# The order of the early second stage and the place of the last weight sums in a fused attention and bilinear kernel

## The chip, the cores and the metric

The kernel runs on one core of a Trainium2 chip. The metric is the device time of one execution in microseconds (us). The profile shows the core's engines: PE (TensorE matmuls), PEld (TensorE weight loads, which overlap the matmuls), DVE (VectorE), ACT (ScalarE), POOL (GpSimd, nearly unused here) and SP (SyncE, which here only issues DMA transfers).

## The reference, cut to what matters

```python
def _attn_ref(x, state):            # x: 8 x 8 x 512 x 64, state: 8 x 8 x 32 x 64
    scores = scale * np.matmul(x, state.transpose(0, 1, 3, 2))
    a = softmax(scores)
    xread = np.matmul(a, state)
    scores2 = scale * np.matmul(state, x.transpose(0, 1, 3, 2))
    a2 = softmax(scores2)
    sread = np.matmul(a2, x)
    return np.concatenate([xread, sread], axis=2)

def _moe_ref(x, w1, w2, w3, w_out):  # x: 4608 x 512
    a = x @ w1
    b = x @ w2
    h = a * b @ w3
    return h @ w_out
```

`softmax` stands for the four lines that subtract the maximum, take the exponential and divide by the sum. Inputs other than `x` and `state` arrive as float64 bits in parts of the program that the change leaves alone.

## The kernel before

All work on one batch of 512 tokens goes through two stages. **Stage 1** works feature tile by feature tile (`FT` = 8 tiles of 128 features): `stage1_sums` issues twelve matmuls on line 311, six for each of the two weight matrices, into a pair of PSUM banks. Then ACT copies one bank out (line 487, or 292 in batch 0), DVE multiplies the copy by the other bank (line 394, or 293), and the product is split into a high and a low part (`split`: ACT line 97 for the high part, DVE line 98 for the low part). That product is what frees the two banks. **Stage 2** multiplies the products by `w34` = w3 w_out, which is kept as `wo["hi"]` and `wo["lo"]`, three matmuls for each pair of tiles (high by low, high by high, low by high).

PSUM has eight banks. Two single banks (`bank()`, tile `ps_o`) serve stage 2. Three pairs (`two_banks()`, tile `ps`) serve stage 1, the attention scores and the w units; a tile of a pool takes a place that an older tile of the same name has left, and waits until the last reader of that tile is done.

Batch 0 runs beside the set-up that converts the weights. Its stage 2 goes by four token tiles of 128. Two of them are taken early: `early_stage2(quarter)` accumulates two feature tiles into `acc[0]` and `acc[1]` (`project`, line 325), in between the feature tiles of stage 1. After that the loop over `tt` stores the two early ones (`store`: ACT line 338 copies a bank out, a DMA sends it) and works out the other two with `stage2`.

Batches 1 to 7 (`quarter_batch`) use a fast scheme for stage 2: seven products of quarters in place of eight, which need sums and differences of blocks of `w34` (the w sums). `combine_weights(k)` makes a quarter of them: two sums on DVE (line 366), four differences into a scratch tile `raw` (line 372), then a split into `t_hi` (ACT line 97) and `t_lo` (DVE line 98). The sums take their scratch from `tmp`, a ring of four buffers that the copies out of PSUM use too. The products of these batches differ from batch 0's: `hidden_quarters` multiplies on line 394 and takes a difference on line 405. Beside stage 1, batch b also works on the attention of batch b + 1: scores (PE line 147), a transpose (DVE line 187), the maximum (line 190), and the softmax.

Two things set the order. PE and SP are scheduled by hand for the whole kernel: their instructions stand as the code issues them. ACT and DVE are scheduled by hand only up to `order.close()`, that is, through the set-up. Behind it a scheduler orders these two by the priority in which the code was written and by its estimate of when inputs are ready; blocks under `tc.high_priority()` (the copies and products of stage 1 and the stores) go ahead. On the chip each engine then runs its instructions in the order of the program. Last of all come the state rows (`state_rows`) of all batches.

Of the kernel before, what the change touches and what calls it, by code (L numbers as in the profile page):

```python
# [36 lines left out]
PLAIN = 1  # L37

@with_exitstack
def attn_bilinear_kernel(  # L40
# [11 lines left out]
    B, _, NT, H, D = x_s.shape  # L52
# [35 lines left out]
    def bank():  # L88
        return ps_o.tile([P, NF], F32, name="ps_o")

    def two_banks():
        return ps_2.tile([P, 2, NF], F32, name="ps_2")

    def split(hi, lo, src):

        return (
            nc.scalar.copy(out=hi, in_=src),  # L97
            nc.vector.tensor_tensor(out=lo, in0=src, in1=hi.bitcast(F32), op=ALU.subtract),  # L98
        )
# [165 lines left out]
    def sw_steps(b):  # L265
        sw_tiles.setdefault(b, {})

        def unit(half, i):
            ps = two_banks()
            as_q = ps.rearrange("p k (c f) -> p k c f", c=2)  # L270
            per_head(as_q, b, lambda rows, j: w_sb[rows, 2 * half:2 * half + 2, i, j])
            sw_tiles[b][half, i] = sw_pair()
            split(*sw_tiles[b][half, i], ps)

        return [(lambda half=half, i=i: unit(half, i)) for half in range(HALF) for i in range(2)]
# [26 lines left out]
    def stage1_sums(b, ft):  # L302
        half, c = divmod(ft * P, NF)
        ps = two_banks()
        hi, lo = at_tiles[b]
        for i in range(2):
            w_hi, w_lo = sw_tiles[b][half, i]
            k = 0
            for kt in range(KT):
                for w, a in ((w_hi, lo), (w_hi, hi), (w_lo, hi)):  # L310
                    nc.tensor.matmul(  # L311
                        ps[:, i], w[:, kt, c:c + P], a[:, kt], start=(k == 0), stop=(k == 3 * KT - 1)
                    )
                    k += 1
        return ps
# [43 lines left out]
    QF = FT // 2  # L359
    HT, HO = S // 2, DO // 2  # L360

    def combine_weights(k):

        raw = [tmp_tile() for _ in range(2)]
        for i, whole in enumerate(raw):
            nc.vector.tensor_tensor(
                out=whole, in0=wo["hi"][:, i * QF + k].bitcast(F32), in1=wo["lo"][:, i * QF + k].bitcast(F32), op=ALU.add
            )
        b11, b12, b21, b22 = (whole[:, half * HO:(half + 1) * HO] for whole in raw for half in range(2))
        t = late.tile([P, QF, S], F32, name="raw")[:, :, :HO]  # L370
        for j, (x, y) in enumerate(((b12, b11), (b22, t[:, 0]), (b22, b12), (b21, t[:, 1]))):
            nc.vector.tensor_tensor(out=t[:, j], in0=x, in1=y, op=ALU.subtract)
        split(t_parts["hi"][:, :, k], t_parts["lo"][:, :, k], t)

    def tmp_tile():
        return main.tile([P, NF], F32, name="tmp", bufs=4)
# [102 lines left out]
    def quarter_batch(b):  # L479
        q = {"raw": []}  # L480
        w = sw_steps(b + 1) if b + 1 < B else [lambda: None] * 4
        softmax = iter(())
        for ft in range(FT):
            ps = stage1_sums(b, ft)
            a_sb = tmp_tile()
            with tc.high_priority():
                nc.scalar.copy(out=a_sb, in_=ps[:, 0])  # L487
            hidden_quarters(a_sb, ps[:, 1], ft, q)
            if ft == 1:
                run([reads[b]])  # L490
                if b + 1 < B:
                    scores, reads[b + 1], _ = attention_steps(b + 1)
                    softmax = scores()
                    next(softmax)
                    load_tokens(b + 1)
                if b + 2 < B:
                    load_x(b + 2)
            elif ft in (2, 4):
                next(softmax, None)
            if b == PLAIN and ft == 1:  # L500
                combine_weights(QF - 1)
        stage2_quarters(b, q, w[:2], [*w[2:], lambda: softmax])

    def run(steps):
# [5 lines left out]
    with tc.tile_pool(name="pro", bufs=2) as pro:  # L510

        places = [w_sb[:, n // 2, n % 2].rearrange("p j f -> p (j f)") for n in range(2 * QT)]
        w_out = [places[(FT + k) // 2][:, k % 2 * DO:(k % 2 + 1) * DO] for k in range(FT)]

        chunks = [places[k % (FT // 2)] for k in range(FT)]
        w3s, w34_ps = {}, {}

        def finish(i):
            split(wo["hi"][:, i], wo["lo"][:, i], w34_ps[i][:, :DO])

        def convert_first(k):
            ends = PARTS.get(k, (NW,))
            return to_f32(pro, w34_k[k], chunks[k], ends, (), wout=w_out[k])

        def w34_first(k):

            for i in range(FT // 2):
                nc.tensor.matmul(
                    w34_ps[i][:, :DO], chunks[k][:, DO + i * P:DO + (i + 1) * P], w_out[k],
                    start=(k == 0), stop=(k == FT - 1),  # L530
                )

        def convert_w3(i):
            w3s[i] = pro.tile([P, NW], F32, name="w3", bufs=2)
            return to_f32(pro, w3t[i - FT // 2], w3s[i])

        def w34(i, ks=range(FT)):
            if ks[0] == 0:
                w34_ps[i] = bank()
            for k in ks:  # L540
                nc.tensor.matmul(
                    w34_ps[i][:, :DO], w3s[i][:, k * P:(k + 1) * P], w_out[k], start=(k == 0), stop=(k == FT - 1)
                )

        def convert_half(n):

            return to_f32(pro, w12[n], places[n])

        def sets(quarter):
            for i in range(2):  # L550
                sw_quarter(0, quarter, i)


        gs, acc, early = [], [], range(2)

        def early_stage2(quarter):
            for tt in early:
                if quarter == 0:
                    acc.append(bank())
                for ft in range(2 * quarter, 2 * quarter + 2):  # L560
                    project(acc[tt], gs, tt, ft)

        order = ctx.enter_context(ExitStack())
        order.enter_context(tc.manual_schedule(engines={mybir.EngineType.Activation, mybir.EngineType.DVE}))
        pair = two_banks()
        w34_ps.update(enumerate([bank(), bank(), pair[:, 0], pair[:, 1]]))
        for k in range(FT + AHEAD):
            run([partial(convert_first, k) if k < FT else partial(convert_w3, k - FT // 2)])
            if k >= AHEAD:
                w34_first(k - AHEAD)  # L570
        load_x(0)
        scores, reads[0], _ = attention_steps(0)
        softmax = scores()
        next(softmax)
        finish(0)
        finish(1)
        split(wo["hi"][:, 2:4], wo["lo"][:, 2:4], pair[:, :, :DO])
        w34(4)

        w1_0, w2_0, w1_1, w2_1 = map(convert_half, range(4))  # L580
        go = lambda steps: next(steps, None)
        w3_6 = convert_w3(6)
        go(w1_0), go(softmax), go(w1_0)
        finish(4)
        go(w2_0), go(w3_6), go(softmax), go(w3_6)
        w34(5)
        go(softmax)
        go(w2_0)
        finish(5)
        w3_7 = convert_w3(7)  # L590
        go(w3_7), go(w3_7), go(w1_1), go(w1_1), go(w2_1), go(w2_1)
        load_tokens(0)
        w34(6)
        sets(0)
        finish(6)
        w34(7, range(LAST))
        sets(1)
        w34(7, range(LAST, FT))
        finish(7)
        order.close()  # L600
        for quarter in range(QT):
            stage1(0, 2 * quarter, gs)
            if quarter == 1:
                run(sw_steps(0)[2:])
            if quarter:
                early_stage2(quarter - 1)
            if quarter == 1:
                side = side_steps()
            elif quarter == 2:
                run(side.pop(0))  # L610
            stage1(0, 2 * quarter + 1, gs)
            if quarter == 0:
                run([partial(convert_half, n) for n in range(4, 2 * QT)])
                load_x(1)
                with tc.issue_after(last_split[1].ins):
                    go(softmax)
        run(side.pop(0))
        early_stage2(QT - 1)
# [3 lines left out]
    for tt in range(NT):  # L622
        dests = [(out[0, tt * P:(tt + 1) * P], 0, P)]
        if tt in early:
            store(acc[tt], dests)
        else:
            stage2(gs, tt, dests)
        run(side[tt])
        if tt + 1 < QF:
            combine_weights(tt)  # L630

    def state_rows():
        n = B * NS
# [74 lines left out]
```

## Time and profile before

| what | us |
|---|---|
| median of 3 runs (lowest, highest) | 494.64 (494.48, 495.07) |
| the profiled execution | 494.89 |
| its span | 493.1 |
| PE busy | 486.8 |
| DVE busy | 375.9 |
| ACT busy | 238.8 |
| batch 1 begins on PE, from the span's start | 120.29 |
| batch 2 begins on PE | 169.40 |
| batch 3 begins on PE | 218.05 |

The span is the time between the first and last instruction that the profiler saw; the device time holds a little more around it. All starts below are counted from the span's start. A row of a timeline gives start, duration, engine, line, operation, output <- inputs, shapes and count; brackets give idle time ahead of the instruction, and what ended it. Matmuls overlap each other, so that a matmul's own duration is longer than the step from one start to the next.

### The profile page before, as it was taken

What the parts mean: (1) busy time and instruction counts of PE and PEld (TensorE: products, weight loads), DVE (VectorE), ACT (ScalarE), POOL (GpSimd) and SP (SyncE); (2) the same over time, 40 slices, a digit from 0 to 9 for tenths busy, and PEclk for the clock granted to TensorE, in tenths of its full rate; (3) what the DMA queues carried; (4) which work ended last, traced back from release to release, by engine and by line L of the source; (5) the groups of instructions that cost most, each with busy time, mean ns of one, the idle gap of its engine ahead of it and who ended that gap; (6) DMA issues with size and microseconds to landing.
All of it is one profiled execution on the core that took longest, in us unless ns stands there. A gap on an engine that the chain in (4) does not pass through costs nothing.

```text
span 493.1 us, 8917 instructions
## 1 busy us (share of the span) xinstructions
PE 486.8 (99%) x3558; PEld 378.4 (77%) x3558; DVE 375.9 (76%) x555; ACT 238.8 (48%) x364; POOL 0.2 (0%) x4
## 2 busy tenths in 40 slices
PE   8999999999999999999999999999999999999996
PEld 6444467777787978797889778977897788899885
DVE  5669897699899579937994899389839983577870
ACT  4777784444357135704560456055505650354650
POOL 0000000000000000000000000000000000000000
PEclk9999999999999999999999999999999999999999
DMA  8996981153113504130413042304220222001001
GB/s 342 359 394 216 366 294 25 19 183 97 34 51 132 128 5 179 39 90 5 179 41 91 5 177 46 85 5 177 49 82 6 87 49 80 6 2 55 33 1 43
DMA packets 56362, 52.50 MB, mean 106 GB/s; under 512 B 42752, under 2 KB 50944, under 8 KB 51712
## 3 DMA queue, kind: packets, MB, share of 16 engines
q1 hardware_dynamic: 47488, 43.27, 26.9%
q10 hardware_dynamic: 8832, 8.65, 5.1%
q8 instruction: 28, 0.46, 0.4%
q14 instruction: 14, 0.11, 0.1%
HBM read 38.27 MB, written 8.91 MB: 96 GB/s over the span
## 4 chain that ended last, share of the span: by engine, by line
PE 77%; DMA 7%; DVE 7%; ACT 5%; SPq 2%; issue 1%; DVEq 0%; ACTq 0%
PE ps L311 30%; PE ps_o L421 25%; PE ps L147 6%; PE ps_o L325 5%; PE ps L421 4%; DMA raw<-in_w_k_dram 3%; PE ps L647 3%; ACT ulps L126 2%; SPq L171 2%; DMA raw<-in_w_dram 2%; PE ps L648 2%; DMA raw<-in_w3t_dram 2%; PE ps_o L243 1%; ACT w_sb L118 1%; DVE work L187 1%
## 5 line engine op out<-in xcount | busy, mean ns | idle before, releaser
L311 PE MATMUL ps<-at_lo,sw_hi 128*128 128x512 f32 x256 | 101.9, 398 | 0.3 <-DVE g_x L394 0.3
L311 PE MATMUL ps<-at_hi,sw_hi 128*128 128x512 f32 x256 | 99.8, 390 | 0.0
L311 PE MATMUL ps<-at_hi,sw_lo 128*128 128x512 f32 x256 | 99.7, 389 | 0.0
L487 ACT COPY tmp<-ps 128x512 f32<-128x512 f32 x56 | 32.8, 587 | 124.5 <-PE ps L311 70.1
L311 PEld LDWEIGHTS ps<-at_lo,sw_hi 128*128 128x128 f32 x256 | 48.1, 188 | 18.7 <-DVE g_x L394 8.1
L311 PEld LDWEIGHTS ps<-at_hi,sw_lo 128*128 128x128 f32 x256 | 48.1, 188 | 10.2
L311 PEld LDWEIGHTS ps<-at_hi,sw_hi 128*128 128x128 f32 x256 | 48.1, 188 | 9.5 <-issue 0.2
L394 DVE TENSOR_TENSOR g_x<-tmp,ps 128x512 f32<-128x512 f32 x28 | 19.1, 683 | 33.3 <-ACT tmp L487 32.8
L98 DVE TENSOR_TENSOR sw_lo<-ps,sw_hi 128x1024 fp32r<-128x1024 f32 (+1 forms) x34 | 38.1, 1154 | 0.2 <-ACT sw_hi L97 0.2
L97 ACT CAST g_hi<-g_x 128x512 fp32r<-128x512 f32 x42 | 26.0, 621 | 21.2 <-PE ps_o L421 13.1
L421 PE MATMUL ps_o<-t_lo,g_hi 128*128 128x256 f32 x168 | 34.5, 287 | 0.0
L421 PE MATMUL ps_o<-wo_lo,g_hi 128*128 128x256 f32 x168 | 34.4, 286 | 0.0
L421 PE MATMUL ps_o<-wo_hi,g_hi 128*128 128x256 f32 x168 | 33.8, 283 | 0.0
L421 PE MATMUL ps_o<-t_hi,g_hi 128*128 128x256 f32 x168 | 33.8, 283 | 0.0
L421 PE MATMUL ps_o<-wo_hi,g_lo 128*128 128x256 f32 x168 | 33.8, 283 | 0.0
L421 PE MATMUL ps_o<-t_hi,g_lo 128*128 128x256 f32 x168 | 33.8, 283 | 0.0
L97 ACT CAST g_hi<-raw 128x512 fp32r<-128x512 f32 x42 | 25.2, 619 | 16.5 <-DVE raw L394 7.8
L98 DVE TENSOR_TENSOR g_lo<-raw,g_hi 128x512 fp32r<-128x512 f32 x42 | 28.8, 689 | 4.6 <-ACT g_hi L97 4.3
L97 ACT CAST sw_hi<-ps 128x1024 fp32r<-128x1024 f32 (+1 forms) x34 | 31.2, 967 | 1.7 <-PE ps L147 1.6
L147 PE MATMUL ps<-w_sb,st 64*32 64x512 f32 (+1 forms) x544 | 31.4, 570 | 0.0
L421 PEld LDWEIGHTS ps_o<-wo_lo,g_hi 128*128 128x128 f32 x168 | 26.6, 191 | 5.6 <-ACT tmp L446 5.0
L421 PEld LDWEIGHTS ps_o<-t_lo,g_hi 128*128 128x128 f32 x168 | 26.1, 192 | 5.0 <-issue 5.0
(109 smaller groups left out, 895.8 us busy)
## 6 DMA issues: line engine op xcount, KB each, us to landing
raw<-in_w_k_dram SPq DMA_DIRECT2D x8, 1024.0 KB, 6.9
x_d<-in_x_d_dram SPq DMA_DIRECT2D x8, 1024.0 KB, 7.5
raw<-in_w_dram SPq DMA_DIRECT2D x8, 1024.0 KB, 6.8
x_s<-in_x_s_dram SPq DMA_DIRECT2D x8, 1024.0 KB, 5.0
out_dram<-tmp ACTq DMA_DIRECT2D x56, 128.0 KB, 1.8
raw<-in_w3t_dram SPq DMA_DIRECT2D x4, 1024.0 KB, 7.6
e<-work SPq DMA_DIRECT2D x112, 32.0 KB, 2.0
sread<-turned SPq DMA_DIRECT2D x128, 4.0 KB, 1.7
```

The source lines that it names most:

```text
L97: nc.scalar.copy(out=hi, in_=src),
L98: nc.vector.tensor_tensor(out=lo, in0=src, in1=hi.bitcast(F32), op=ALU.subtract),
L126: nc.scalar.activation(out=ulps[:, part], in_=low.bitcast(U32), func=AF.Copy, scale=2.0**-29)
L147: nc.tensor.matmul(ps[j * NS:(j + 1) * NS, q], sts[b][rows, j], moving(rows, j), start=True, stop=True)
L171: nc.sync.dma_start(out=dest(slice(c * NS, (c + 1) * NS), j), in_=src(slice(j * NS, (j + 1) * NS), c))
L311: nc.tensor.matmul(ps[:, i], w[:, kt, c:c + P], a[:, kt], start=(k == 0), stop=(k == 3 * KT - 1))
L325: nc.tensor.matmul(ps[:, :DO], g, wo[w][:, ft, :], start=(ft == 0 and k == 0), stop=(ft == FT - 1 and k == 2))
L394: nc.vector.tensor_tensor(out=whole, in0=a, in1=b, op=ALU.mult)
L421: nc.tensor.matmul(ps[:, tt * HO:(tt + 1) * HO], g[:, tt * P:(tt + 1) * P], w(part, k), start=(fresh and k == 0 and n == 0 and tt == 0), s ...
L487: nc.scalar.copy(out=a_sb, in_=ps[:, 0])
L647: nc.tensor.matmul(ps[:, i], wh[:, ks], sr[:, kt], start=(kt == 0), stop=False)
L648: nc.tensor.matmul(ps[:, i, :n], wl[:, ks], sr[:, kt, 1], start=False, stop=(kt == NP - 1))
```

## The change

The change has two edits. In `early_stage2` the loop over the two token tiles goes inside the loop over feature tiles, and both banks are taken ahead of the loops. And `combine_weights(QF - 1)`, the last quarter of the w sums, which was called in batch 1 behind feature tile 1, is called in the loop over token tiles of batch 0, where the other three quarters are.

```diff
@@ quarter_batch
             elif ft in (2, 4):
                 next(softmax, None)
-            if b == PLAIN and ft == 1:
-                combine_weights(QF - 1)
         stage2_quarters(b, q, w[:2], [*w[2:], lambda: softmax])
@@ early_stage2
         def early_stage2(quarter):
-            for tt in early:
-                if quarter == 0:
-                    acc.append(bank())
-                for ft in range(2 * quarter, 2 * quarter + 2):
+            if quarter == 0:
+                acc.extend(bank() for _ in early)
+            for ft in range(2 * quarter, 2 * quarter + 2):
+                for tt in early:
                     project(acc[tt], gs, tt, ft)
@@ the loop over token tiles of batch 0
         run(side[tt])
-        if tt + 1 < QF:
-            combine_weights(tt)
+        combine_weights(tt)
```

On PE, feature tiles 4 and 5 in early stage 2. `ps_o_544` is `acc[0]`; `ps_o_551` before and `ps_o_545` after are `acc[1]`. `g_hi_591` and `g_lo_592` are the parts of tile 4, `g_hi_652` and `g_lo_653` those of tile 5. Before, up to the first reader of `g_lo_653`:

```order
L325 MATMUL ps_o_544<-wo_lo_94,g_hi_591 128x512
L325 MATMUL ps_o_544<-wo_hi_93,g_hi_591 128x512
L325 MATMUL ps_o_544<-wo_hi_93,g_lo_592 128x512
L325 MATMUL ps_o_544<-wo_lo_94,g_hi_652 128x512
L325 MATMUL ps_o_544<-wo_hi_93,g_hi_652 128x512
L325 MATMUL ps_o_544<-wo_hi_93,g_lo_653 128x512
```

And now, on the same engine at the same place:

```order
L325 MATMUL ps_o_544<-wo_lo_94,g_hi_591 128x512
L325 MATMUL ps_o_544<-wo_hi_93,g_hi_591 128x512
L325 MATMUL ps_o_544<-wo_hi_93,g_lo_592 128x512
L325 MATMUL ps_o_545<-wo_lo_94,g_hi_591 128x512
L325 MATMUL ps_o_545<-wo_hi_93,g_hi_591 128x512
L325 MATMUL ps_o_545<-wo_hi_93,g_lo_592 128x512
L325 MATMUL ps_o_544<-wo_lo_94,g_hi_652 128x512
L325 MATMUL ps_o_544<-wo_hi_93,g_hi_652 128x512
L325 MATMUL ps_o_544<-wo_hi_93,g_lo_653 128x512
```

The first reader of `g_lo_653` moved from the sixth matmul to the ninth.

On PE, tiles 6 and 7 in early stage 2 (`g_x_672` and `g_x_703`, each holding both parts) and the first matmul of token tile 2 (`ps_o_865`, which takes the bank of `ps_o_544`). Before:

```order
L325 MATMUL ps_o_544<-wo_lo_94,g_x_672 128x512
L325 MATMUL ps_o_544<-wo_hi_93,g_x_672 128x512 x2
L325 MATMUL ps_o_544<-wo_lo_94,g_x_703 128x512
L325 MATMUL ps_o_544<-wo_hi_93,g_x_703 128x512 x2
L325 MATMUL ps_o_551<-wo_lo_94,g_x_672 128x512
L325 MATMUL ps_o_551<-wo_hi_93,g_x_672 128x512 x2
L325 MATMUL ps_o_551<-wo_lo_94,g_x_703 128x512
L325 MATMUL ps_o_551<-wo_hi_93,g_x_703 128x512 x2
L325 MATMUL ps_o_865<-wo_lo_94,g_hi_420 128x512
```

And now:

```order
L325 MATMUL ps_o_544<-wo_lo_94,g_x_672 128x512
L325 MATMUL ps_o_544<-wo_hi_93,g_x_672 128x512 x2
L325 MATMUL ps_o_545<-wo_lo_94,g_x_672 128x512
L325 MATMUL ps_o_545<-wo_hi_93,g_x_672 128x512 x2
L325 MATMUL ps_o_544<-wo_lo_94,g_x_703 128x512
L325 MATMUL ps_o_544<-wo_hi_93,g_x_703 128x512 x2
L325 MATMUL ps_o_545<-wo_lo_94,g_x_703 128x512
L325 MATMUL ps_o_545<-wo_hi_93,g_x_703 128x512 x2
L325 MATMUL ps_o_865<-wo_lo_94,g_hi_420 128x512
```

The last matmul into `ps_o_544` moved from the sixth place to the ninth of twelve, three ahead of the matmul that needs its bank instead of six.

On DVE, the first products of batch 1. `ps_2_958` and `ps_2_983` are feature tiles 0 and 1, `ps_2_1084` is tile 2, `ps_2_1058` the scores; `raw_923` belongs to the third quarter of the w sums and `raw_1077` to the last. Before, the stretch around tile 2's product:

```order
L366 TENSOR_TENSOR tmp_1073<-wo_hi_93,wo_lo_94 128x512
L366 TENSOR_TENSOR tmp_1074<-wo_hi_93,wo_lo_94 128x512
L372 TENSOR_TENSOR raw_1077<-tmp_1073 128x256
L372 TENSOR_TENSOR raw_1077<-tmp_1074,tmp_1073 128x256
L372 TENSOR_TENSOR raw_1077<-tmp_1074,raw_1077 128x256
L187 STREAM_TRANSPOSE work_1101<-ps_2_1058 128x1024
L394 TENSOR_TENSOR g_x_1099<-tmp_1097,ps_2_1084 128x512
L372 TENSOR_TENSOR raw_1077<-tmp_1074,raw_1077 128x256
L190 TENSOR_REDUCE m2_1103<-ps_2_1058 128x2
L98 TENSOR_TENSOR t_lo_795<-raw_1077,t_hi_794 128x4x256
```

And now, from the third quarter's `t_lo` on, where `ps_2_969` and `ps_2_994` are tiles 0 and 1 and `raw_962` belongs to the last quarter; its first sum (into `tmp_958`) stands just ahead of this piece:

```order
L98 TENSOR_TENSOR t_lo_795<-raw_923,t_hi_794 128x4x256
L366 TENSOR_TENSOR tmp_959<-wo_hi_93,wo_lo_94 128x512
L372 TENSOR_TENSOR raw_962<-tmp_958 128x256
L372 TENSOR_TENSOR raw_962<-tmp_959,tmp_958 128x256
L394 TENSOR_TENSOR g_x_984<-tmp_982,ps_2_969 128x512
L372 TENSOR_TENSOR raw_962<-tmp_959,raw_962 128x256 x2
L98 TENSOR_TENSOR t_lo_795<-raw_962,t_hi_794 128x4x256
L394 TENSOR_TENSOR g_x_984<-tmp_1007,ps_2_994 128x512
```

The last quarter's sums moved from behind the product of tile 1 to ahead of it, its `t_lo` with them. The transpose on line 187, the reduction on line 190 and tile 2's product now follow each other in this order. In the built program tile 4 of batch 1 takes the banks of tile 2 in both kernels; tile 5 takes those of tile 3 before, and those of the scores now.

## The prediction

> **What bounds the kernel now.** I read the page's busy times first, then the chain that ended last, then the waits of PE (TensorE) alone.
>
> ```profile
> PE 486.8 (99%) x3558; PEld 378.4 (77%) x3558; DVE 375.9 (76%) x555; ACT 238.8 (48%) x364; POOL 0.2 (0%) x4
> PE 77%; DMA 7%; DVE 7%; ACT 5%; SPq 2%; issue 1%; DVEq 0%; ACTq 0%
> PE ps_o L325 <- DVE g_lo L98: 0.3, 1, 0.3
> PE ps L311 <- DVE g_x L394: 0.3, 1, 0.3
> ```
>
> PE is the bound. Its work is the same before and after the change, so only its waits count. Behind the set-up the view of waits shows two, and each edit touches one: line 325 waits for a low part in early stage 2, and line 311 waits for a product in batch 1. A DVE or ACT instruction that moves costs nothing until PE waits for it. The chain in order of time shows what the second wait is worth:
>
> ```profile
> 120.29 5.45 PE ps L311 x24
> 169.40 5.47 PE ps L311 x24
> 218.05 5.46 PE ps L311 x24
> ```
>
> These are the starts of batches 1, 2 and 3. Batch 1 takes 49.11 us and batch 2 48.65, so batch 1 loses 0.46 more than a steady batch. The last row also gives PE's step: 24 matmuls in 5.46 us are 0.2275 us from start to start.
>
> **The first edit: tiles outermost in early stage 2.** The timelines of PE and DVE at feature tiles 4 and 5:
>
> ```profile
> 96.12 0.40 PE L325 MATMUL ps_o<-wo_hi,g_hi 128*128 128x512 f32 x1
> 96.85 0.50 PE L325 MATMUL ps_o<-wo_hi,g_lo 128*128 128x512 f32 x1 [0.34 <-DVE g_lo L98]
> 97.19 0.39 PE L325 MATMUL ps_o<-wo_lo,g_hi 128*128 128x512 f32 x1
> 96.11 0.68 DVE L98 TENSOR_TENSOR g_lo<-tmp,g_hi 128x512 fp32r<-128x512 f32 x1
> ```
>
> The matmul at 96.12 is the fifth of twelve. The sixth needs the low part of tile 5, which DVE ends at 96.79. From 96.12 to 97.19 there should be two steps, 0.455, but there are 1.07: the stop costs 0.61, of which 0.11 is the slower restart (0.34 from the first matmul to the second). After the change the low part of tile 5 is first read by the ninth matmul, at 96.12 + 4 × 0.2275 = 97.03, behind 96.79. **Gain 0.61.**
>
> The same edit moves the end of the first accumulator. At tiles 6 and 7:
>
> ```profile
> 104.13 0.65 DVE L98 TENSOR_TENSOR g_x<-tmp,g_x 128x512 fp32r<-128x512 f32 x1
> 104.29 0.50 PE L325 MATMUL ps_o<-wo_lo,g_x 128*128 128x512 f32 x1
> 107.14 0.39 PE L325 MATMUL ps_o<-wo_lo,g_hi 128*128 128x512 f32 x1
> 106.04 0.59 ACT L338 COPY tmp<-ps_o 128x512 f32<-128x512 f32 x1 [0.50 <-PE ps_o L325]
> ```
>
> The row at 107.14 opens token tile 2 in the bank that `acc[0]` leaves. `acc[0]` was complete after six of twelve matmuls, and its copy ended at 106.63, 0.51 before that row. Now it is complete after nine, 3 × 0.2275 = 0.68 later, and the slack of 0.51 becomes a wait of 0.17, with a restart 0.28. **Loss 0.28**: a bank takes the place of the low part. The low part of tile 7 (104.13 + 0.65 = 104.78) is first read by the seventh matmul instead of the fourth; even 0.61 earlier that is 104.29 + 0.11 + 6 × 0.2275 - 0.61 = 105.15, so nothing stops there. Net, PE comes out of batch 0 0.33 us earlier. If the ACT copy were later for another reason, all of the 0.33 could go; if it came at once, 0.61 would stay.
>
> DVE gains less. Its product of tile 7 waited for a copy that PE's lateness delayed:
>
> ```profile
> 100.80 1.23 DVE L216 TENSOR_TENSOR work<-work,sum 128x1024 f32<-128x1024 f32 x1
> 102.17 0.69 DVE L293 TENSOR_TENSOR tmp<-tmp,ps 128x512 f32<-128x512 f32 x1
> 101.55 0.59 ACT L292 COPY tmp<-ps 128x512 f32<-128x512 f32 x1 [2.61 <-PE ps L311]
> ```
>
> The copy ended at 102.14, now 101.53. An operation on 1024 columns lets the next one start 1.14 us after it (the row at 134.78 and the one behind it, below), so the product can start at 101.94: **0.23 earlier**, no more, and DVE then works almost without a gap. The bounds are 0 and 0.61.
>
> **The second edit: the last quarter of the w sums.** It removes and adds no instruction; it moves four microseconds of DVE work ahead of batch 1's products. The order of instructions decides the rest. Before, on DVE, ACT and PE:
>
> ```profile
> 119.72 0.68 DVE L366 TENSOR_TENSOR tmp<-wo_hi,wo_lo 128x512 f32<-128x512 f32 x1
> 120.32 0.76 DVE L372 TENSOR_TENSOR raw<-tmp 128x256 f32<-128x256 f32 x2
> 122.99 1.23 DVE L98 TENSOR_TENSOR t_lo<-raw,t_hi 128x1024 fp32r<-128x1024 f32 x1 [1.12 <-ACT t_hi L97]
> 124.52 0.69 DVE L394 TENSOR_TENSOR g_x<-tmp,ps 128x512 f32<-128x512 f32 x1 [0.30 <-ACT tmp L487]
> 126.38 0.69 DVE L394 TENSOR_TENSOR g_x<-tmp,ps 128x512 f32<-128x512 f32 x1 [1.17 <-ACT tmp L487]
> 132.68 0.65 DVE L394 TENSOR_TENSOR g_x<-tmp,ps 128x512 f32<-128x512 f32 x1
> 133.25 0.41 DVE L372 TENSOR_TENSOR raw<-tmp,raw 128x256 f32<-128x256 f32 x1
> 133.58 1.22 DVE L190 TENSOR_REDUCE m<-ps 128x2 f32<-128x1024 f32 x1
> 134.78 1.23 DVE L98 TENSOR_TENSOR t_lo<-raw,t_hi 128x1024 fp32r<-128x1024 f32 x1
> 135.92 0.68 DVE L394 TENSOR_TENSOR g_x<-tmp,ps 128x512 f32<-128x512 f32 x1
> 133.05 0.39 PE L311 MATMUL ps<-at_hi,sw_lo 128*128 128x512 f32 x1
> 133.39 0.50 PE L311 MATMUL ps<-at_lo,sw_hi 128*128 128x512 f32 x1
> 136.66 0.50 PE L311 MATMUL ps<-at_lo,sw_hi 128*128 128x512 f32 x1 [0.26 <-DVE g_x L394]
> 137.00 0.40 PE L311 MATMUL ps<-at_hi,sw_hi 128*128 128x512 f32 x1
> ```
>
> The four rows of line 394 are the products of tiles 0 to 3, and each frees two banks. Tile 4 of PE starts at 133.39, 0.06 behind the end of tile 2's product; tile 5 at 136.66, 0.06 behind tile 3's. In the changed program tile 4 again takes the banks of tile 2, while tile 5 takes those of the scores. So the deciding time is the end of tile 2's product, 132.68 + 0.65 = 133.33 before. Three things move it:
>
> - Ahead of it now stand the last `raw` difference, the reduction on line 190 and the last `t_lo`, which stood behind it: 0.33 + 1.13 + 1.14 = 2.60 later (the reduction at the 1.13 of its size, since the `t_lo` behind it was itself waiting).
> - DVE's idle time ahead of it was 1.12 + 0.30 + 1.17 = 2.59. Now the first w sum of the last quarter stands in the 1.12 (0.60, from 119.72 to 120.32) and leaves 0.52; the 0.30 and the 1.17 are filled with work. But the last conversion has the chain of the third, differences on DVE, `t_hi` on ACT, `t_lo` on DVE, with nothing queued between: 1.12 again. Idle left 1.64, so 0.95 earlier.
> - DVE itself comes 0.23 earlier.
>
> 133.33 + 2.60 - 0.95 - 0.23 = 134.75, and PE starts tile 4 at 134.81. Without a wait it would be there at 133.05 + 0.23 - 0.33 = 132.95: a wait of nearly 1.9 us, which swallows the gain of the first edit whole. Behind the waiting matmul stand all of PE's later matmuls. Tile 5 follows at 134.81 + 0.11 + 12 × 0.2275 = 137.65 without a wait, if the scores' banks are free by then. ACT's exponentials read them last:
>
> ```profile
> 137.17 0.68 ACT L197 ACTIVATE e<-ps,m 128x512 f32<-128x512 f32 x1
> 138.41 0.20 ACT L197 ACTIVATION_READ_ACCUMULATOR e<-ps,m 128x1 f32 x1
> ```
>
> The pair takes 1.44 us. In the changed order it waits only for the small operation behind tile 2's product, so it ends near 136.3, ahead of 137.65. Before, tile 5 ran as if from 137.00 - 0.23 = 136.77. **Net +0.88 us.** Behind it neither kernel waits in batch 1, DVE has the sums behind it, and the later batches keep their 48.65.
>
> Bounds: were the sum not to fit into the 1.12 (0.60) and DVE not earlier (0.23), +1.71. Were the second 1.12 covered by other work, -0.24.
>
> **Sum.** The profiled execution took 494.89 us (span 493.1), 0.25 above the median of 494.64. 494.89 + 0.88 = 495.77; against the median 495.52. I take 495.5. A change under 0.2% (0.99 us) can't be told from none here.
>
> **Rivals.**
>
> *Batch 1 becomes a steady batch (faster).* There tile 4 hardly waits:
>
> ```profile
> 182.57 0.50 PE L311 MATMUL ps<-at_lo,sw_hi 128*128 128x512 f32 x1
> 181.84 0.67 DVE L394 TENSOR_TENSOR g_x<-tmp,ps 128x512 f32<-128x512 f32 x1
> ```
>
> In batch 2 PE also starts 0.06 behind the product of tile 2. Without the sums in its midst batch 1 could fall to 48.65: -0.46 and -0.33 make -0.79, 493.85 by the median. It needs tile 2's product done by 132.9, 1.85 earlier than I count; DVE's order speaks against it, since the last `t_lo` stands between the products of tiles 0 and 1. Chance 0.14, 0.05 of it beyond 0.2%.
>
> *The two sides cancel.* If DVE is 0.9 less late, the loss is nil: 494.6. Chance 0.07. The first edit failing in its own place belongs to the forecast, for its gain is swallowed: +1.11 (DVE not earlier).
>
> *The wait of nearly 1.9 us slows PE's clock (slower).* Its place is tile 4 of batch 1.
>
> ```profile
> 130.00:140.00 10.00, 9.74 (x43) 7.46 (x42) 10.00 (x15) 4.86 (x10) 0.00 (x0) 1.00 0.05 7
> ```
>
> The granted clock (third number from the end) stayed 1.00 over the stop at 136.66, a third of this one. At half the clock, tile 4's twelve matmuls alone would take 12 × 0.2275 = 2.73 more: +3.61, 498.25. It decides from where a stop is long enough; no row has one of this length. Chance 0.05. The Trainium skill ("TensorE: Matmul & The Clock Gate", section "A second HAM failure mode: psum-queue depth-cycling") speaks against such a change: short idle times of PE between groups that cycle through PSUM banks made its clock fall back in another kernel. By its Part 1 the drop takes an idle window of about 3.4 us; by that the clock stays.
>
> **How the numbers follow.** Forecast 0.74, reaching from 494.4 to 496.35 (-0.24 to +1.71); its centre of 0.88 is near 0.99, so 0.32 of it is slower by over 0.2% and 0.42 within. With the rivals: faster 0.05, within 0.42 + 0.09 + 0.07 = 0.58, slower 0.32 + 0.05 = 0.37. The range 494.3 to 496.4 leaves out the first rival and the clock, 0.19.
>
> **What would show it.** Right: no wait of line 325 for the low part of tile 5; a stop of about 0.3 at the first matmul of token tile 2, behind ACT line 338; a stop of 1.5 to 2 us at tile 4 of batch 1, behind line 394; none at tile 5; batch 2 starting about 0.9 later than 169.40. Wrong: line 394 of tile 2 ending before 133.5, DVE idle under 1 us ahead of the last `t_lo`, or a later batch longer than 48.65.

## The result and the profile after

| kernel | median us | lowest, highest | runs |
|---|---|---|---|
| before | 494.57 | 494.01, 495.53 | 19 |
| after | 495.37 | 494.96, 496.46 | 19 |

The ratio is 1.0015, with a 95% interval from 1.0008 to 1.0021: the change costs 0.8 us. That is less than the 0.2% (0.99 us) below which the prediction counts a change as none, but more than nothing, since the interval leaves out 1. The forecast was 495.5. The profiled execution of the kernel after took 495.37 us, with a span of 493.6.

The page's busy times and the view of PE's waits, of the kernel after (a wait's row gives the total, the number of times and the longest, in us):

```profile
PE 486.7 (99%) x3558; PEld 378.4 (77%) x3558; DVE 376.0 (76%) x555; ACT 239.0 (48%) x364; POOL 0.2 (0%) x4
PE ps L311 <- DVE g_x L394: 1.1, 1, 1.1
```

The busy times are those of before. The wait of line 325 for the low part has left the list, and that of line 311 for a product has grown from 0.3 to 1.1 us; it is now the wait of another tile. The chain in order of time, of the kernel after (start, duration, what):

```profile
134.35 11.18 PE ps L311 x48
169.81 5.47 PE ps L311 x24
218.47 5.47 PE ps L311 x24
```

The chain now enters batch 1's first stage at 134.35, tile 4, and not at 136.66, tile 5. Batch 2 starts 0.41 later than before (169.81 against 169.40), and the steady batch still takes 48.66. That is less than the 0.8 of the medians, because the two profiled executions differ already in the set-up; the one before took 494.89, 0.32 above its median. A DVE reduction in batch 0 that stands ahead of every stop that the change touches shows by how much:

```profile
92.09 1.19 DVE L190 TENSOR_REDUCE m<-ps 128x2 f32<-128x1024 f32 x1
91.73 1.19 DVE L190 TENSOR_REDUCE m<-ps 128x2 f32<-128x1024 f32 x1
```

The first row is before, the second after: DVE was 0.36 earlier in the second execution. This row is the **DVE mark** below. Counted from it, batch 2 starts 0.41 + 0.36 = 0.77 us later, in line with the medians.

The first edit, in the timelines of PE and DVE of the kernel after:

```profile
96.62 0.39 PE L325 MATMUL ps_o<-wo_hi,g_hi 128*128 128x512 f32 x1
96.85 0.39 PE L325 MATMUL ps_o<-wo_hi,g_lo 128*128 128x512 f32 x1
95.76 0.69 DVE L98 TENSOR_TENSOR g_lo<-tmp,g_hi 128x512 fp32r<-128x512 f32 x1
105.88 0.61 PE L325 MATMUL ps_o<-wo_hi,g_x 128*128 128x512 f32 x2
105.91 0.59 ACT L338 COPY tmp<-ps_o 128x512 f32<-128x512 f32 x1 [1.15 <-PE ps_o L325]
106.54 0.50 PE L325 MATMUL ps_o<-wo_lo,g_hi 128*128 128x512 f32 x1
106.88 0.40 PE L325 MATMUL ps_o<-wo_hi,g_hi 128*128 128x512 f32 x1
```

The first reader of tile 5's low part is the ninth matmul, at 96.85; the part is ready at 95.76 + 0.69 = 96.45, and PE keeps its even step. At the hand-over ACT's copy of `acc[0]` ends at 106.50, and the first matmul of token tile 2 starts at 106.54 in place of 105.88 + 2 × 0.2275 = 106.33: a stop of 0.21 and a restart of 0.11 (0.34 to the second matmul instead of 0.2275).

The second edit, in the timeline of DVE and then of PE:

```profile
122.41 1.23 DVE L98 TENSOR_TENSOR t_lo<-raw,t_hi 128x1024 fp32r<-128x1024 f32 x1 [0.52 <-ACT t_hi L97]
124.82 0.68 DVE L394 TENSOR_TENSOR g_x<-tmp,ps 128x512 f32<-128x512 f32 x1
127.41 1.23 DVE L98 TENSOR_TENSOR t_lo<-raw,t_hi 128x1024 fp32r<-128x1024 f32 x1 [1.11 <-ACT t_hi L97]
128.56 0.68 DVE L394 TENSOR_TENSOR g_x<-tmp,ps 128x512 f32<-128x512 f32 x1
132.52 1.19 DVE L190 TENSOR_REDUCE m<-ps 128x2 f32<-128x1024 f32 x1
133.63 0.67 DVE L394 TENSOR_TENSOR g_x<-tmp,ps 128x512 f32<-128x512 f32 x1
132.84 0.39 PE L311 MATMUL ps<-at_hi,sw_lo 128*128 128x512 f32 x1
134.35 0.50 PE L311 MATMUL ps<-at_lo,sw_hi 128*128 128x512 f32 x1 [1.12 <-DVE g_x L394]
134.69 0.39 PE L311 MATMUL ps<-at_hi,sw_hi 128*128 128x512 f32 x1
137.20 0.39 PE L311 MATMUL ps<-at_lo,sw_hi 128*128 128x512 f32 x1
```

The idle times ahead of the two `t_lo` are 0.52 and 1.11. The product of tile 2 ends at 134.30. PE would have begun tile 4 at 132.84 + 0.23 = 133.07 and begins at 134.35, a stop of 1.28 and a restart of 0.11. (The bracket gives 1.12, since it counts from the end of the matmul ahead, which is modelled.) Tile 5 follows at 137.20 without a wait.

### The profile page after: what moved, and what is told of

Read it like the earlier page. It is cut to its first block, busy times and chain, and to the rows that moved or that the text cites. A ratio compares the mean times of both kernels' runs of the same rounds, so it can differ in the third digit from the quotient of the medians.

```text
span 493.6 us, 8920 instructions
## 1 busy us (share of the span) xinstructions
PE 486.7 (99%) x3558; PEld 378.4 (77%) x3558; DVE 376.0 (76%) x555; ACT 239.0 (48%) x364; POOL 0.2 (0%) x4
## 4 chain that ended last, share of the span: by engine, by line
PE 78%; DVE 11%; ACT 5%; DMA 3%; SPq 2%; issue 1%; ACTq 0%; DVEq 0%
PE ps L311 29%; PE ps_o L421 25%; PE ps L147 6%; PE ps L421 4%; PE ps L644 3%; PE ps_o L526 3%; PE ps L526 3%; PE ps_o L325 2%; SPq L171 2%; PE ps L645 2%; ACT ulps L126 1%; DMA raw<-in_w_dram 1%; ACT w_sb L118 1%; PE ps_o L243 1%; DVE raw L372 1%; DMA raw<-in_w_k_dram 1%
```

## The experiments

All results in one place; "before" is the kernel before on the same chip. The ratio is that of the comparison with before and need not equal that of the two medians. The last two columns are from each kernel's profile and count to the first matmul of batch 2 (169.24 before, 169.65 after; the chain's rows above start 0.16 behind it). One counts from the DVE mark, the other from the first matmul of batch 1 (120.12 before, 119.70 after). The first is the right measure where DVE decides when batch 2 starts, the second where PE does. The changed kernel was measured in one session and is compared below with runs of others; the kernel before agrees in all of them within 0.1.

| kernel | median us (runs) | before | ratio, 95% interval | DVE mark to batch 2 | batch 1 to batch 2 |
|---|---|---|---|---|---|
| before | | 494.57 | | 77.15 | 49.12 |
| after | 495.37 (19) | 494.57 | 1.0015, 1.0008 to 1.0021 | 77.92 | 49.95 |
| first edit alone | 494.68 (11) | 494.59 | 0.9999, 0.9991 to 1.0008 | 77.19 | 49.12 |
| the same again | 494.43 (11) | 494.57 | 1.0005, 0.9996 to 1.0013 | 76.96 | 49.12 |
| second edit alone | 495.63 (11) | 494.59 | 1.0017, 1.0009 to 1.0026 | 78.20 | 50.12 |
| after, tiles 6 and 7 in the old order | 495.32 (11) | 494.59 | 1.0025, 1.0013 to 1.0038 | 77.93 | 50.37 |
| after, last split later | 494.63 (11) | 494.59 | 0.9997, 0.9988 to 1.0006 | 76.81 | 49.02 |
| after, scores later | 494.25 (11) | 494.49 | 0.9999, 0.9990 to 1.0007 | 76.90 | 48.84 |
| after, a reduction twice | 495.45 (11) | 494.49 | 1.0018, 1.0009 to 1.0027 | 77.90 | 50.11 |
| first edit, tiles 6 and 7 in the old order | 494.04 (11) | 494.57 | 0.9993, 0.9984 to 1.0002 | 76.59 | 49.13 |
| before, reduction behind tile 2 | 493.18 (7) | 494.49 | 0.9968, 0.9957 to 0.9979 | 77.17 | 49.11 |
| after, three things together | 491.91 (5) | 494.49 | 0.9948, 0.9935 to 0.9960 | 76.32 | 48.32 |

**The second edit alone.** The early second stage goes back to the old order:

```diff
-            if quarter == 0:
-                acc.extend(bank() for _ in early)
-            for ft in range(2 * quarter, 2 * quarter + 2):
-                for tt in early:
+            for tt in early:
+                if quarter == 0:
+                    acc.append(bank())
+                for ft in range(2 * quarter, 2 * quarter + 2):
                     project(acc[tt], gs, tt, ft)
```

> The second edit alone: early stage 2 goes token tiles outermost as before. Theory, that DVE's order decides and PE's gain from the first edit is swallowed: the wait for the low part of tile 5 in early stage 2 is back (0.6 us on PE), the product of tile 2 in batch 1 ends only 0.23 later than in the changed kernel, the stop ahead of tile 4 of batch 1 is about 0.1 shorter than there, and the time is 0.2 us above the changed kernel (495.6 against 495.37; +1.0 to +1.1 against before). Rival, that PE's sum counts in full: 0.33 above the changed kernel (495.7).

Measured: 495.63, 0.26 above the changed kernel; from the mark, 0.28. The two ratio intervals overlap, so the medians alone don't show the 0.26; and it lies between the 0.23 of DVE and the 0.33 of PE, and by itself tells neither. The timelines of DVE and then of PE, of this kernel:

```profile
100.83 1.22 DVE L216 TENSOR_TENSOR work<-work,sum 128x1024 f32<-128x1024 f32 x1
102.25 0.69 DVE L293 TENSOR_TENSOR tmp<-tmp,ps 128x512 f32<-128x512 f32 x1 [0.19 <-ACT tmp L292]
96.89 0.50 PE L325 MATMUL ps_o<-wo_hi,g_lo 128*128 128x512 f32 x1 [0.41 <-DVE g_lo L98]
135.02 0.50 PE L311 MATMUL ps<-at_lo,sw_hi 128*128 128x512 f32 x1 [1.50 <-DVE g_x L394]
```

DVE's product of tile 7 starts 102.25 - 100.83 = 1.42 behind the operation ahead of it, since it waits for the copy again; in the changed kernel the two starts are 1.15 apart (100.44 and 101.59). So the first edit brings DVE 0.27 here, and that is the whole 0.28 from the mark. On PE the wait of early stage 2 is back. The stop at tile 4 is longer than in the changed kernel, not the 0.1 shorter that was expected: in this execution the product of tile 2 came 0.66 later (0.40 at the mark, 0.27 from tile 7), and PE's last matmul of tile 3 only 0.29 later (133.13 against 132.84).

**Tiles 6 and 7 in the old order.** In the changed kernel, the last quarter of early stage 2 goes token tiles outermost:

```diff
-            for ft in range(2 * quarter, 2 * quarter + 2):
-                for tt in early:
-                    project(acc[tt], gs, tt, ft)
+            fts = range(2 * quarter, 2 * quarter + 2)
+            pairs = [(tt, ft) for tt in early for ft in fts] if quarter == QT - 1 else [(tt, ft) for ft in fts for tt in early]
+            for tt, ft in pairs:
+                project(acc[tt], gs, tt, ft)
```

> The changed kernel, with tiles 6 and 7 of early stage 2 going token tiles outermost again, so that acc[0] is complete after six of twelve matmuls. Theory: the wait at the first matmul of token tile 2 goes and PE leaves batch 0 0.28 us earlier than in the changed kernel, but the stop ahead of tile 4 of batch 1 becomes 0.28 longer (about 1.7 instead of 1.4), and the time is that of the changed kernel (0.0, within 0.1 us). Rival, that PE's gain reaches the end: 0.28 us below the changed kernel.

Measured: 495.32, -0.05 against the changed kernel, and 0.01 from the mark. PE's timeline:

```profile
132.20 0.39 PE L311 MATMUL ps<-at_hi,sw_lo 128*128 128x512 f32 x1
134.32 0.50 PE L311 MATMUL ps<-at_lo,sw_hi 128*128 128x512 f32 x1 [1.73 <-DVE g_x L394]
```

PE arrives 0.64 earlier than in the changed kernel (132.20 against 132.84) and stops 0.61 longer: it waits for the product all the same. Batch 1 takes PE 50.37 instead of 49.95, and from the DVE mark nothing changes. This shows that what PE gains at the hand-over is swallowed, as forecast. That PE gained more than 0.28 is taken up in the last section. The runs of this kernel spread more widely than the others (494.95 to 497.75); the profile is of a run of 495.32 and doesn't show why.

**The split of the last quarter behind tile 2's product.** The sums stay; `t_hi` and `t_lo` of the last quarter are issued in batch 1 and held back on both engines:

```diff
@@ combine_weights(k, hold=False)
-        split(t_parts["hi"][:, :, k], t_parts["lo"][:, :, k], t)
+        if hold:
+            held.append(t)
+        else:
+            split(t_parts["hi"][:, :, k], t_parts["lo"][:, :, k], t)
@@ quarter_batch
+            if b == PLAIN and ft == 2:
+                with tc.issue_after(product_of[0].ins), tc.issue_after(copied.ins):
+                    split(t_parts["hi"][:, :, QF - 1], t_parts["lo"][:, :, QF - 1], held[0])
```

> The changed kernel, with only the split of the last quarter (its t_hi and t_lo, about 1.2 us of DVE and the idle time ahead of it) moved from between the products of tiles 0 and 1 of batch 1 to behind the product of tile 2; its sums stay where the change put them. Theory, that what stands ahead of tile 2's product on DVE decides: that product ends near 132.8 instead of 134.3, the stop ahead of tile 4 of batch 1 goes or shrinks below 0.3, and the time is 1.2 to 1.6 us below the changed kernel, 0.5 to 0.8 below before (493.8 to 494.1). Rival, that the place of the split does not matter and another wait (a bank, the state tiles, the scores) holds tile 4: the stop stays above 1 us and the time is within 0.3 of the changed kernel.

Measured: 494.63 (493.92 to 495.51), 0.74 below the changed kernel and 0.04 above before; from the mark, 1.11 below the changed kernel. The stop at tile 4 shrank as forecast, but the time gained less than forecast. DVE's and PE's timelines (this kernel's product is on line 397):

```profile
131.20 1.19 DVE L190 TENSOR_REDUCE m<-ps 128x2 f32<-128x1024 f32 x1
132.31 1.20 DVE L204 TENSOR_REDUCE m<-work 128x32 f32<-128x1024 f32 x1
133.43 0.68 DVE L397 TENSOR_TENSOR g_x<-tmp,ps 128x512 f32<-128x512 f32 x1
133.73 0.39 PE L311 MATMUL ps<-at_hi,sw_lo 128*128 128x512 f32 x1
134.16 0.50 PE L311 MATMUL ps<-at_lo,sw_hi 128*128 128x512 f32 x1
```

The product starts 133.43 - 92.65 = 40.78 behind the mark, against 133.63 - 91.73 = 41.90 in the changed kernel. What left the stretch ahead of it is a `t_lo` (1.14) with its idle time (1.11); what came in is the reduction on line 204 (1.12), which the scheduler now put ahead of the product: 41.90 - 1.14 - 1.11 + 1.12 = 40.77. The sum by DVE's order holds to 0.01, and the expectation was wrong by the reduction that it left out. In this execution the mark was also 0.92 later than in that of the changed kernel, and with it the wait for tile 5's low part was back (0.41). Why the medians show 0.74 and not 1.11 stays open: a mark as late as this in most of its runs would explain it, but one profile doesn't show that.

**The scores one tile later.** The first DVE work that the scores of batch 1 bring then stands behind tile 2's product:

```diff
             if ft == 1:
                 run([reads[b]])
+            if ft == (2 if b == PLAIN else 1):
                 ...
-            elif ft in (2, 4):
+            elif ft in ((3, 4) if b == PLAIN else (2, 4)):
                 next(softmax, None)
```

> The changed kernel, with the scores of batch 1 issued one feature tile later (behind tile 2 instead of tile 1) and the softmax steps behind tiles 3 and 4. On DVE the product of tile 2 then stands ahead of the transpose and the reduction (2.3 us), with the t_lo still between tiles 0 and 1; tile 5 takes the banks of tile 3. Theory, that what stands ahead of tile 2's product on DVE decides: that product ends about 132.0 instead of 134.3, no stop ahead of tile 4, a stop of about 0.3 ahead of tile 5, since the transpose and two reductions now stand ahead of tile 3's product; time 1.0 us below the changed kernel (494.4). Rival, that DVE's total up to tile 3 decides and not the order: the stop moves to tile 5 in full and the time is within 0.3 of the changed kernel.

Measured: 494.25, 1.12 below the changed kernel; from the mark, 1.02. DVE's and PE's timelines:

```profile
131.31 0.68 DVE L394 TENSOR_TENSOR g_x<-tmp,ps 128x512 f32<-128x512 f32 x1
135.64 0.39 PE L311 MATMUL ps<-at_hi,sw_lo 128*128 128x512 f32 x1
136.02 0.50 PE L311 MATMUL ps<-at_lo,sw_hi 128*128 128x512 f32 x1
```

The product of tile 2 ends at 131.99 (forecast 132.0). Nothing stops ahead of tile 4; ahead of tile 5 136.02 - 135.64 - 0.23 = 0.15 is left (forecast 0.3). Of the 1.39 that the stop and its restart cost, 0.15 and a restart remain, which leaves 1.13. The load on DVE is the same; less of it stands ahead of tile 2's product. (On PE the scores also move behind tile 2, and tile 5 takes the banks of tile 3.)

**A reduction twice.** More DVE work, right behind the deciding product:

```diff
             nc.vector.tensor_reduce(out=m1, in_=s1v, axis=AX.X, op=ALU.max)
+            if b == PLAIN + 1:
+                nc.vector.tensor_reduce(out=m1, in_=s1v, axis=AX.X, op=ALU.max)
```

> The changed kernel, with the reduction on line 204 for batch 2's softmax, which stands right behind tile 2's product on DVE, done twice (the second time with the same result): about 1.12 us more DVE work in batch 1, behind the product that decides. Theory: the stop ahead of tile 4 is as in the changed kernel, none ahead of tile 5, the time is the same (0.0, within 0.1 us). Rival, that the load on DVE in batch 1 counts and not its order: up to 1.1 us slower (496.5).

Measured: 495.45 against 495.37; from the mark, 0.02 less than the changed kernel. The DVE timeline of this kernel (lines from 206 on are two further down here), and in the last two rows that of the changed kernel:

```profile
134.82 0.67 DVE L396 TENSOR_TENSOR g_x<-tmp,ps 128x512 f32<-128x512 f32 x1
135.48 1.20 DVE L204 TENSOR_REDUCE m<-work 128x32 f32<-128x1024 f32 x1
136.71 1.22 DVE L206 TENSOR_REDUCE m<-work 128x32 f32<-128x1024 f32 x1
137.85 0.68 DVE L396 TENSOR_TENSOR g_x<-tmp,ps 128x512 f32<-128x512 f32 x1
138.44 1.22 DVE L207 TENSOR_TENSOR work<-work,m 128x1024 f32<-128x1024 f32 x1
135.53 1.23 DVE L205 TENSOR_TENSOR work<-work,m 128x1024 f32<-128x1024 f32 x1
136.67 0.68 DVE L394 TENSOR_TENSOR g_x<-tmp,ps 128x512 f32<-128x512 f32 x1
```

The second reduction doesn't push tile 3's product back. It takes the place of the subtraction on line 207 (205 in the changed kernel), which now follows that product: from tile 2's product to tile 3's there are 3.03 here (137.85 - 134.82) and 3.04 in the changed kernel (136.67 - 133.63). So 1.1 us more DVE work in batch 1 cost nothing; whether a later product of tile 3 would cost something was not tried.

**The first edit alone.** The last quarter of the w sums goes back into batch 1:

```diff
@@ quarter_batch
+            if b == PLAIN and ft == 1:
+                combine_weights(QF - 1)
@@ the loop over token tiles of batch 0
-        combine_weights(tt)
+        if tt + 1 < QF:
+            combine_weights(tt)
```

> The first edit alone: the last quarter of the w sums stays in batch 1, behind feature tile 1. Theory: line 325 has no wait for the low part of tile 5, a wait of about 0.17 stands at the first matmul of token tile 2, and PE leaves batch 0 0.33 us earlier than before; but the products of tiles 2 and 3 of batch 1 still decide, and DVE is only 0.23 earlier, so the time is 0.2 us below before (494.3 to 494.4 against 494.57), with the stop ahead of tile 5 of batch 1 still there and that ahead of tile 4 about 0.1 longer. Rival, that PE's own gain decides: 0.33 to 0.6 us below before.

Measured: 494.68 against 494.59. It took 0.1 more, not 0.2 less, though both lie inside the interval. The DVE timeline shows where DVE's 0.23 went:

```profile
126.73 0.69 DVE L394 TENSOR_TENSOR g_x<-tmp,ps 128x512 f32<-128x512 f32 x1 [1.45 <-ACT tmp L487]
```

The product of tile 1 waits 1.45 for ACT's copy, where it waited 1.17 before. That copy follows PE, not DVE. So with the last quarter in batch 1, DVE's lead is lost again at this product, and PE sets the pace. In this execution the first matmul on tiles 4 and 5 came at 95.85 instead of 95.21 from the set-up, 0.64 late, with the mark only 0.31 late. A PE that is 0.33 later against DVE would have stopped 0.33 less in the old order as well, so there was little left for the first edit to gain. Two further runs were made on this reading.

> The first edit alone once more, on the same chip as the kernel above, as its measure. By the DVE sum that was made for it first: 0.23 below before. By PE's pace, as its profile showed it: between 0.0 and 0.3 below before, 0.0 where the set-up hands PE over 0.6 later than in the profile of before, as it did in its profile.

Measured: 494.43 against 494.57, 0.14 below, while the ratio (1.0005) lies above 1; the times can't tell the two expectations apart. The profiles can. In this one batch 1 begins 0.38 earlier on PE than before (119.74 against 120.12), the product of tile 1 starts 0.38 earlier (126.00 against 126.38), and so does batch 2 (168.86 against 169.24). In the first profile of this kernel batch 1 began 0.35 later than before (120.47), and batch 2 0.35 later (169.59). So PE's pace decides here, and the mark is no measure for this kernel. (In the kernel before, PE itself waits for DVE in early stage 2, so there the mark does carry over to batch 2.)

The other has the order of tiles 6 and 7 of the run above, on the first edit alone.

> The first edit alone, with tiles 6 and 7 of early stage 2 token tiles outermost again, so that acc[0] is complete after six of twelve matmuls; the last quarter of the w sums in batch 1. The profile of the first edit alone showed that DVE, where it came earlier, only waited longer for the copy of tile 1 of batch 1, which follows PE. Theory from that: with the last quarter in batch 1, PE's own pace decides, and the 0.28 that the hand-over no longer costs reaches the end, 0.28 us below the first edit alone, where the same edit in the changed kernel gave 0.05. Rival, that DVE's earlier work decides here too: 0.0 against the first edit alone.

Measured: 494.04 (493.92 to 494.57), 0.39 below the first edit alone on the same chip (494.32 to 495.17). The same edit that gave 0.05 with the last quarter behind batch 0 gives 0.39 with it in batch 1. The profiles show 0.20 of it: batch 1 begins 0.20 earlier on PE (119.54 against 119.74) and batch 2 0.19 earlier, though the mark is 0.18 later. The rest of the 0.39 is not shown there. That bears out the reading: in the changed kernel DVE decides, in the kernel before PE's pace does. The table says the same. With the last quarter in batch 1, five profiles take 49.11 to 49.13 from batch 1 to batch 2 on PE, however early PE comes. In the changed kernel and the one with tiles 6 and 7 in the old order it is the time from the mark that stays (77.92, 77.93), and that on PE does not (49.95, 50.37). Against before itself this kernel (0.9993, 0.9984 to 1.0002) can't be told from no change.

**The reduction behind tile 2's product in every batch.** The steady batches lose 0.15 and a restart at tile 4, and there the reduction on line 204 stands ahead of the product. In the kernel before (`product_of` holds the newest product of line 394, and `issue_after` puts what stands under it behind that product):

```diff
-            nc.vector.tensor_reduce(out=m1, in_=s1v, axis=AX.X, op=ALU.max)
+            with tc.issue_after(product_of[0].ins) if product_of else ExitStack():
+                nc.vector.tensor_reduce(out=m1, in_=s1v, axis=AX.X, op=ALU.max)
```

> The kernel before, with one thing: the reduction on line 204 stands behind tile 2's product in batches 2 to 7 (in batch 1 it stood there already). Theory, that the stop of 0.15 ahead of tile 4 and its restart of 0.11 in each steady batch comes from the place of that reduction: batches take 48.4 instead of 48.65 and the time is 1.3 to 1.6 us below before (493.0 to 493.3). Rival, that something else holds tile 4: 0.0 against before.

Measured: 493.18 against 494.49, 1.31 less, interval 0.9957 to 0.9979. DVE and PE in batch 2, where the product is on line 395 and the reduction on line 205, and the starts of batches 3 and 4:

```profile
180.67 0.68 DVE L395 TENSOR_TENSOR g_x<-tmp,ps 128x512 f32<-128x512 f32 x1
181.27 1.21 DVE L205 TENSOR_REDUCE m<-work 128x32 f32<-128x1024 f32 x1
181.95 0.39 PE L312 MATMUL ps<-at_hi,sw_lo 128*128 128x512 f32 x1
182.18 0.39 PE L312 MATMUL ps<-at_lo,sw_hi 128*128 128x512 f32 x1
217.34 0.40 PE L312 MATMUL ps<-at_lo,sw_hi 128*128 128x512 f32 x1
265.69 0.40 PE L312 MATMUL ps<-at_lo,sw_hi 128*128 128x512 f32 x1
```

Tile 4 starts one step behind tile 3, and the batch takes 48.35. The reduction moved in batches 2 to 6; five times 0.30 make 1.5, for 1.31 by the medians (1.0 to 2.1 by the interval). The expectation had counted 0.26 a batch.

**Three things together.** The last run combines the later split, the old order of tiles 6 and 7, and the reduction behind tile 2's product, on the changed kernel; its edits are those shown.

> The changed kernel with three things: the split of the last quarter behind tile 2's product as in the run that moved only the split; tiles 6 and 7 of early stage 2 token tiles outermost; and the reduction on line 204 behind tile 2's product in every batch (before it stood ahead of it in batches 2 to 7, and in that run in batch 1 too). Theory: no stop ahead of tile 4 in batch 1, worth 1.39 against the changed kernel, 0.28 more from the hand-over in batch 0, and in batches 1 to 6 with a stop of 0.15 and its restart of 0.11 the 0.26 goes, six times 1.6 us: batches of 48.4 instead of 48.65, in all about 3.2 us below the changed kernel (492.2). Rival, that the stop in a steady batch has another cause, such as the restart behind the scores: batches stay at 48.65 and the time is 1.4 to 1.7 below (493.7 to 494.0).

Measured: 491.91 (491.67 to 492.17) against 494.49, interval 0.9935 to 0.9960. Its batch 2 starts 77.92 - 76.32 = 1.60 sooner than that of the changed kernel (forecast 1.39 + 0.28), and its steady batch takes 48.35 (216.01 to 264.36). Where the product goes ahead of the reductions, the second edit pays; this version is ahead of both kernels.

## Why the prediction held

**Edit 1.** The gain at tile 5's low part and the loss at the hand-over came as forecast: the even step at 96.85 (the twelve matmuls took 0.64 less, 0.61 forecast), and 0.21 + 0.11 = 0.32 for the forecast 0.28. PE began batch 1 0.42 earlier than before, 0.17 of it from the set-up (95.04 against 95.21), so 0.25 for the forecast 0.33. The loss was larger than its two parts: from tile 6 to the end of this stage PE took 0.38 longer, since some matmuls behind the restart came at steps of 0.23 to 0.24.

**Edit 2.** DVE's order decided. The idle times of 0.52 and 1.12 came as 0.52 and 1.11, and the product of tile 2 ended at 134.30 for 134.75; with the mark 0.36 earlier, 0.09 is left. The scores' banks were free in time: ACT was done with them at 135.86, ahead of tile 5 at 137.20. That what stands ahead of this product counts was shown from both sides: 2.3 us of DVE work moved behind it brings 1.0 to 1.1 (all that PE had to gain but the small stop at tile 5), 1.1 us added behind it costs nothing.

**The swallowed gain.** Shown by the run with tiles 6 and 7 in the old order: PE earlier by 0.64, time the same.

**The stop at tile 4.** It was 1.28 where nearly 1.9 were forecast, of which 0.36 is the mark, 0.09 the product and 0.12 PE's later arrival (a stop on line 243, see the last section). The time follows the product and not the length of the stop, so the net of 0.88 measured 0.80 by the medians and 0.77 from the mark. Two of the signs named in the prediction, a stop of 1.5 to 2 us and batch 2 about 0.9 later, thus did not show as named (1.28 and 0.41); in both, the earlier mark of the second execution is the larger part of the difference.

**What was wrong** is a step that the sum took for granted: that the 0.23 of DVE (0.27 in these profiles) and the 0.33 of PE are fixed sizes. They hang on how far DVE and PE are apart when the set-up ends, and that varies by some tenths between executions. The expectation for the first edit alone also carried DVE's 0.23 over to a kernel in which PE sets the pace. The prediction also misread its comparison for the clock: the stop at tile 5 before is 136.66 - 136.01 - 0.23 = 0.42, under a quarter of the 1.86 forecast and not a third.

**The rivals.** Batch 1 did not become steady and the sides did not cancel. A batch 1 as short as a steady one came only with the three things together (on PE from 119.35 to 167.67, 48.32). The clock, in the kernel after and then in that with tiles 6 and 7 in the old order:

```profile
130.00:140.00 10.00, 8.88 (x40) 7.03 (x39) 9.96 (x17) 5.62 (x11) 0.00 (x0) 1.00 0.05 7
130.00:140.00 10.00, 8.27 (x37) 6.51 (x36) 9.97 (x17) 5.60 (x11) 0.00 (x0) 1.00 0.05 6
```

The granted clock (third number from the end) stayed at 1.00 over the stop of 1.28, and in the second over one of 1.89 (134.32 - 132.20 - 0.23), as long as the prediction had it. The rule of the Trainium skill ("TensorE: Matmul & The Clock Gate", section "A second HAM failure mode: psum-queue depth-cycling"), that frequent short idle times between groups can pull the clock down, did not show here; these are single stops, which don't test it.

## What to carry to other kernels

Where two engines share a few banks, find the one product that frees the next banks, and count what stands ahead of it on its engine, idle times included; work behind it cost nothing here. Moving work "earlier" on an engine without spare time ahead of that product moves the product later. A gain on the engine that waits is worth nothing as long as it waits for the same thing at the next stop.

## What the runs showed that was not expected

The steady batches held more than the change was about: a reduction of 1.2 us ahead of tile 2's product makes each of five batches 0.30 us longer, and moving it brought 1.31 us.

PE has another stop in waiting between batch 0 and tile 4. The 64 small matmuls on line 243 need blocks that a DVE transpose and a row of DMA transfers bring. The first row is before, the second after:

```profile
125.66 1.10 PE L243 MATMUL ps_o<-x_s,e 128*32 128x64 f32 x64
125.23 1.32 PE L243 MATMUL ps_o<-x_s,e 128*32 128x64 f32 x64
```

After, they took 0.22 longer. In the second profile of the first edit alone the wait is named:

```profile
PE ps_o L243 <- DMA e<-work: 0.3, 1, 0.3
```

In the run with tiles 6 and 7 in the old order this stretch is absent (1.10 again). That is 0.21 of the 0.64 by which PE came earlier there; the other 0.43 it had when batch 1 began (119.27 against 119.70), 0.04 of it from the set-up and 0.39 from the hand-over, where 0.28 had been counted. Why the matmuls on line 243 did not stop in that run was not tried. In the second profile of the first edit alone the stop did not reach batch 2: those at tiles 4 and 5 became shorter by about as much.

The set-up scatters by more than the effects studied: the DVE mark lies between 91.35 and 92.94 in the twelve profiles. In before and after it follows, through a transpose, the landing of block transfers. Where DVE decides, comparing starts from this mark brought the profiles within 0.1 of the medians, but for the later split; where PE decides, the start of batch 1 on PE is the place to count from.
